# Keeping 1+elu in six of eight hidden pairs and subtracting the weights' sum per output tile

## The chip, the core and the metric

The kernel runs on one core of a Trainium2 chip. The metric is the device time of one execution in microseconds. The engines are called by the profile's names: PE (matrix multiply), PEld (its weight loads), DVE (VectorE), ACT (ScalarE), POOL (GpSimd), SP (the queue that issues the DMAs).

## The reference, cut to what matters

Two small attention steps between 32 inducing points and 4 batches of 12480 tokens of width 128 give a new token array. A feed-forward layer of hidden width 2048 follows, with ELU between its two products:

```python
h = x @ w_in                                              # 49920 x 128 by 128 x 2048
g = np.where(h > 0.0, h, alpha * (np.exp(np.minimum(h, 0.0)) - 1.0))   # elu, alpha = 1
return (g @ w_out).astype(np.float32)                     # 2048 x 128
```

Everything is float32. The feed-forward layer is nearly all of the kernel's time.

## The kernel before

Tokens are cut into blocks: 25 per batch, 15 of 512 tokens and 10 of 480 (`GROUPING`), 100 in all. The hidden width is 16 chunks of 128; two chunks are a pair, and a unit is one pair of one block, so a block is 8 units, cp 0 to cp 7. All 800 units run through one software pipeline, in which each engine's order for PE, DVE and ACT is the order of the code (`tc.manual_schedule`); POOL's and SP's instructions are placed by a scheduler. In loop step n:

- `ffn_in(n)` (L612): two PE matmuls of the unit into a two-bank PSUM tile `ph` (three such tiles rotate). A row of ones in the operand makes this h+1. ACT then writes e = exp(ph-1).
- `ffn_mid(n-1)` (L629): DVE writes g = min(max(ph, 1), e), which is 1+elu(h). For letter D it goes back into `ph`, otherwise into `e`.
- `ffn_split(n-1)` (L636): for P and D, ACT writes `gh`, the reduced-precision (fp32r) copy of g-1.
- `ffn_low(n-2)` (L643): the rest gl = (g-1) - gh. For D one DVE instruction does both; for P, POOL first takes 1 from e (L653) and then takes gh away (L658). For N there is no split, and POOL only takes 1 from e (L653).
- `ffn_out(n-5)` (L660): the second product into the PSUM tile `po` of the block. A split pair takes six fp32r matmuls (gh by `wo_h`, gh by `wo_l`, gl by `wo_h`, for each of two chunks), an N pair two matmuls of full float32 (e by `wo_n`), which the profile records as four. After a block's last unit DVE transposes `po` into `o` (L688), and SP sends it out in four DMAs.

The letters are in `PLAN`, one for each cp: "PDNPDPND". So unit cp 2's second product stands in loop step cp 7 of the same block, and cp 6's in step cp 3 of the next. `gh` and `gl` have four buffers each, `e` five. The steps of the attention for the next blocks and for the next batch (the side work: `scores`, `weights_of`, `gather`, `attend_*`) are put between units at places that fixed numbers give. Before unit 0, and interleaved with units 0 to 12, the weights are taken apart and split into `wo_h`, `wo_l` and `wo_n`.

Of the kernel before, what the change touches and what calls it, by code (L numbers as in the profile page):

```python
# [9 lines left out]
F32 = mybir.dt.float32  # L10
F32R = mybir.dt.float32r
I32 = mybir.dt.int32
U32 = mybir.dt.uint32
AF = mybir.ActivationFunctionType
ALU = mybir.AluOpType
AX = mybir.AxisListType

P = 128
Q = 32
TM = 512  # L20
# [4 lines left out]

PLAN = "PDNPDPND"

# [13 lines left out]
def kernel(  # L45
# [8 lines left out]
    nc = tc.nc  # L54
    B, N, C = x.shape
# [18 lines left out]
    NFC = F // P  # L74
    NCP = NFC // 2
    assert len(PLAN) == NCP
    CHUNKS_S = [f for f in range(NFC) if PLAN[f // 2] != "N"]
    CHUNKS_N = [f for f in range(NFC) if PLAN[f // 2] == "N"]
    WHERE_S = {f: i for i, f in enumerate(CHUNKS_S)}
    WHERE_N = {f: i for i, f in enumerate(CHUNKS_N)}  # L80
    NSPLIT = len(CHUNKS_S)
    SCALE = 1.0 / math.sqrt(C)
# [10 lines left out]
    const = ctx.enter_context(tc.tile_pool(name="const", bufs=1))  # L93
# [4 lines left out]
    ep = ctx.enter_context(tc.tile_pool(name="ep", bufs=2))  # L98
# [7 lines left out]
    op = ctx.enter_context(tc.tile_pool(name="op", bufs=2))  # L106
# [8 lines left out]
    def bank(name, take=False):  # L115
        if not steady and not take:
            return ps_h.tile([P, 2, 512], F32, tag="ph", name=name)[:, 0]
        t = ps_o.tile([P, 512], F32, tag=f"po{turn[0] % 2}", name=name)
        if take:
            turn[0] += 1  # L120
        return t
# [6 lines left out]
        out=fold, in_=ident.rearrange("p (c m) -> p m c", m=Q), axis=AX.X, op=ALU.add  # L128
    )
    sel4 = const.tile([P, 4, Q], F32, name="sel4")  # L130
    for c in range(4):
# [6 lines left out]
        out=mine, in_=ident.rearrange("p (c m) -> p c m", m=Q), axis=AX.X, op=ALU.add  # L138
# [5 lines left out]
    ps = bank("ps_ind")  # L144
# [6 lines left out]
    wo_n = const.tile([P, len(CHUNKS_N), C], F32, name="wo_n")  # L151
    wo_h = const.tile([P, NSPLIT, C], F32R, name="wo_h")
    wo_l = const.tile([P, NSPLIT, C], F32R, name="wo_l")
    WS = 512
    rebias = const.tile([P, 1], F32, name="rebias")
    nc.gpsimd.memset(rebias, -896.0)
# [5 lines left out]
    class Weight:  # L162
# [8 lines left out]
        def take_apart(self):  # L171
            self.part = op.tile([P, WS], U32, tag="o", name="w_part")
            self.scale = self.part.bitcast(F32)
            nc.vector.tensor_scalar(
                out=self.part, in0=self.hi, scalar1=20, scalar2=0x7FF,
                op0=ALU.logical_shift_right, op1=ALU.bitwise_and,
            )
            nc.scalar.activation(self.low, self.lo, AF.Copy, scale=2.0**-52)
# [37 lines left out]
    def load_w_in(half):  # L216
        n = F // 2
        raw = hwp.tile([P, 2 * n], U32, tag="hw", name="w_raw")
        nc.sync.dma_start(raw, w_in[:, 2 * half * n : 2 * (half + 1) * n])
        return [Weight(raw[:, i : i + 2 * WS]) for i in range(0, 2 * n, 2 * WS)]  # L220

    WC = WS // C

    def load_w_out(part, pool, tag):
        raw = pool.tile([P, WC, 2 * C], U32, tag=tag, name="w_raw")
        rows = w_out[part * WS : (part + 1) * WS, :]
        dma = nc.sync.dma_start(raw, rows.rearrange("(c p) d -> p c d", p=P))
        return Weight(raw.rearrange("p c d -> p (c d)")), dma
# [379 lines left out]
    def plan(n):  # L608
        b, k, cp = units[n]
        return PLAN[cp]  # L610

# [24 lines left out]
    def ffn_split(n):  # L636
        v, how = live[n], plan(n)
        shape = list(v["e"].shape)
        if how != "N":
            v["gh"] = ghp.tile(shape, F32R, tag="gh", name=f"gh_{n}")  # L640
            nc.scalar.activation(v["gh"], v["g"], AF.Copy, bias=-1.0)  # L641

    def ffn_low(n):  # L643
        v, how = live[n], plan(n)
        shape = list(v["e"].shape)
        if how == "D":
            v["gl"] = glp.tile(shape, F32R, tag="gl", name=f"gl_{n}")
            nc.vector.scalar_tensor_tensor(  # L648
                out=v["gl"], in0=v["g"], scalar=-1.0, in1=v["gh"].bitcast(F32),
                op0=ALU.add, op1=ALU.subtract,  # L650
            )
        else:
            nc.gpsimd.tensor_scalar(  # L653
                out=v["e"], in0=v["e"], scalar1=-1.0, scalar2=1.0, op0=ALU.add, op1=ALU.mult
            )
        if how == "P":
            v["gl"] = glp.tile(shape, F32R, tag="gl", name=f"gl_{n}")
            nc.gpsimd.tensor_sub(v["gl"], v["e"], v["gh"].bitcast(F32))  # L658

    def ffn_out(n):  # L660
        b, k, cp = units[n]
        v, how = live.pop(n), plan(n)
        T = BLOCKS[k][1]
        U = T // Q
        if cp == 0:
            outs[b, k] = bank(f"po_{b}_{k}", take=True)
        po = outs[b, k]
        parts = []
        for i in range(2):
            f = 2 * cp + i  # L670
            if how == "N":
                parts.append((0, wo_n[:, WHERE_N[f], :], v["e"][:, i]))
            else:
                w = WHERE_S[f]
                parts.append((1, wo_h[:, w, :], v["gh"][:, i]))
                parts.append((1, wo_l[:, w, :], v["gh"][:, i]))
                parts.append((2, wo_h[:, w, :], v["gl"][:, i]))
        parts.sort(key=lambda v: v[0])
        for i, (_, w, g) in enumerate(parts):
            nc.tensor.matmul(  # L680
                po[:, :T], w, g,
                start=(cp == 0 and i == 0),
                stop=(cp == NCP - 1 and i == len(parts) - 1),
            )
        if cp == NCP - 1:
            yield 1
            o = op.tile([P, U, Q], F32, tag="o", name=f"o_{b}_{k}")
            nc.vector.transpose(o.rearrange("p u d -> p (u d)"), po[:, :T])  # L688
            at = b * N + BLOCKS[k][0]
            dst = out[at : at + T, :]  # L690
            for dq in range(4):
                nc.sync.dma_start(
                    dst[:, dq * Q : (dq + 1) * Q].rearrange("(u t) d -> t u d", t=Q),
                    o[dq * Q : (dq + 1) * Q, :, :],
                )
# [45 lines left out]
    def first_batch(b):  # L741
# [8 lines left out]
        win += load_w_in(1)  # L750
        wout = [load_w_out(i, *[(xqp, "xq"), (xmp, "xm")][i // 2]) for i in range(F // WS)]
        steps = {}
# [21 lines left out]
        for s, w in enumerate(win + [w for w, _ in wout]):  # L774
            steps[f"A{s}"], steps[f"C{s}"] = w.take_apart, w.put_together
            steps[f"B{s}"] = lambda w=w, s=s: w.scale_of(s >= 6)
            if s < len(win):
                steps[f"D{s}"] = lambda w=w, s=s: w.finish(win_sb[:, s * WS : (s + 1) * WS])
            else:
# [69 lines left out]
    last = len(units)  # L849
    ffn_mid(last - 1)  # L850
    ffn_split(last - 1)
    ffn_low(last - 2)
    ffn_low(last - 1)
    for n in range(done, last):
        begin(last + n, lambda: ffn_out(n))
        for r in list(running):
            go_on(r, last + n + 1)
# [32 lines left out]
```

## Time and profile before

| | |
|---|---|
| runs, us | 1713.06, 1710.11, 1712.89 (median 1712.89) |
| profiled execution, its own time from first to last instruction | 1710.8 us |
| PE / PEld / DVE / ACT / POOL busy | 97 / 69 / 89 / 81 / 78 % |
| granted PE clock, mean | 0.986 |

The profile gives no other time for the profiled execution than its span; it lies inside the range of the runs. Busy shares are means over a start of about 140 us, in which weights are prepared, and a long even stretch after it, so the prediction reads the even stretch by itself. A row of the timeline has start, duration, engine, line and tiles; PE's matmuls overlap each other, so what one costs is read from start to start and not from its duration.

### The profile page before, as it was taken

The page shows a single profiled execution, that of the slowest core. Times are in us where ns is not written, and L with a number is a line of the kernel's source. Part 1 is how long each engine was busy: PE and PEld are TensorE (multiplying, and loading weights), DVE is VectorE, ACT ScalarE, POOL GpSimd, SP SyncE. Part 2 cuts the span into 40 slices and gives each one's busy share as a digit, 9 for nine tenths or more (in the row PEclk, how much of TensorE's full clock was granted, in tenths as well). Part 3 has the DMA queues.
Part 4 walks back from the last instruction along what each step waited for, and adds up shares of the span by engine and source line. Part 5 has one row for each costly group of instructions (what it writes and reads, how often), then busy time and mean ns, then how long its engine had stood idle before and what let it go on. Part 6 is the DMA issues. An engine that isn't in the chain of part 4 may idle for free.

```text
span 1710.8 us, 22335 instructions
## 1 busy us (share of the span) xinstructions
PE 1656.3 (97%) x7448; PEld 1176.5 (69%) x7448; DVE 1522.5 (89%) x1575; ACT 1390.6 (81%) x1620; POOL 1342.3 (78%) x948
## 2 busy tenths in 40 slices
PE   6589999999999999999999999999999999999998
PEld 4356776677776776767776676677777677777776
DVE  5799899898899998988989999889888989998996
ACT  4378888888787888888888888888878888888886
POOL 4488787787797877877888787787778888888886
PEclk9699999999999999999999999999999999999999
DMA  7144223322324233232223332321222111111111
GB/s 249 35 91 80 56 43 78 63 48 70 70 46 83 37 75 70 45 62 58 71 64 54 65 62 53 75 55 21 74 49 40 35 20 36 28 37 19 36 25 19
DMA packets 384754, 98.10 MB, mean 57 GB/s; under 512 B 364864, under 2 KB 370784, under 8 KB 384384
## 3 DMA queue, kind: packets, MB, share of 16 engines
q1 hardware_dynamic: 384640, 96.68, 27.9%
q8 instruction: 59, 0.97, 0.2%
q14 instruction: 55, 0.45, 0.1%
HBM read 48.94 MB, written 25.56 MB: 44 GB/s over the span
## 4 chain that ended last, share of the span: by engine, by line
PE 87%; DVE 7%; ACT 3%; issue 2%; DMA 1%; POOL 0%; SPq 0%; DVEq 0%; ACTq 0%
PE po L680 62%; PE ph L618 20%; ACT e L626 2%; DVE e L632 1%; PE ps_s L312 1%; PE ps_t L531 1%; PE ps_hh L403 1%; DVE ph L632 1%; ACT gh L641 1%; DMA xm<-in_x_dram 1%; DVE o L688 1%; DVE w_part L198 1%; DVE gl L648 0%; DMA w_raw<-in_moe_w_in_dram 0%; PE ps_hw L467 0%
## 5 line engine op out<-in xcount | busy, mean ns | idle before, releaser
L626 ACT ACTIVATE e<-ph 128x1024 f32<-128x1024 f32 (+1 forms) x800 | 803.4, 1005 | 228.8 <-PE ph L618 223.7
L653 POOL TENSOR_SCALAR e<-e 128x1024 f32<-128x1024 f32 (+1 forms) x500 | 510.8, 1029 | 280.6 <-ACT gh L641 270.4
L658 POOL TENSOR_TENSOR gl<-e,gh 128x1024 fp32r<-128x1024 f32 (+1 forms) x300 | 703.8, 2346 | 16.8
L632 DVE SCALAR_TENSOR_TENSOR e<-ph,e 128x1024 f32<-128x1024 f32 (+1 forms) x500 | 594.5, 1189 | 88.0 <-ACT e L626 84.9
L618 PE MATMUL ph<-stk,hw 128*128 128x512 f32 (+1 forms) x1600 | 566.8, 436 | 15.8 <-DVE e L632 9.6
L680 PE MATMUL po<-gh,wo_h 128*128 128x512 f32 (+1 forms) x1200 | 469.2, 391 | 7.5 <-ACT wo_h L238 3.5
L680 PE MATMUL po<-gh,wo_l 128*128 128x512 f32 (+1 forms) x1200 | 469.3, 391 | 6.6 <-POOL wo_l L239 6.6
L618 PEld LDWEIGHTS ph<-stk,hw 128*128 128x128 f32 x1600 | 295.4, 189 | 188.9 <-issue 84.9
L632 DVE SCALAR_TENSOR_TENSOR ph<-ph,e 128x1024 f32<-128x1024 f32 (+1 forms) x300 | 359.3, 1198 | 63.1 <-ACT e L626 62.3
L680 PE MATMUL po<-gl,wo_h 128*128 128x512 f32 (+1 forms) x1200 | 371.1, 390 | 0.7 <-POOL gl L658 0.7
L680 PE MATMUL po<-e,wo_n 128*128 128x512 f32 (+1 forms) x800 | 367.8, 582 | 0.1
L648 DVE SCALAR_TENSOR_TENSOR gl<-ph,gh 128x1024 fp32r<-128x1024 f32 (+1 forms) x300 | 356.3, 1188 | 1.0 <-ACT gh L641 1.0
L641 ACT ACTIVATE gh<-e 128x1024 fp32r<-128x1024 f32 (+1 forms) x300 | 311.3, 1038 | 13.9 <-DVE e L632 13.5
L641 ACT ACTIVATE gh<-ph 128x1024 fp32r<-128x1024 f32 (+1 forms) x300 | 300.6, 1002 | 19.1 <-DVE ph L632 18.2
L680 PEld LDWEIGHTS po<-gh,wo_h 128*128 128x128 f32 x1200 | 225.9, 188 | 56.6 <-issue 7.4
L680 PEld LDWEIGHTS po<-gh,wo_l 128*128 128x128 f32 x1200 | 225.9, 188 | 56.5 <-POOL wo_l L239 8.2
L680 PEld LDWEIGHTS po<-gl,wo_h 128*128 128x128 f32 x1200 | 225.6, 188 | 49.1 <-POOL gl L658 1.7
L680 PEld LDWEIGHTS po<-e,wo_n 128*128 128x128 f32 x800 | 150.6, 189 | 106.3 <-issue 91.3
L688 DVE STREAM_TRANSPOSE o<-po 128x512 f32<-128x512 f32 (+1 forms) x100 | 69.1, 691 | 4.0 <-PE po L680 4.0
L259 DVE STREAM_TRANSPOSE xT<-xq 128x1024 f32<-128x1024 f32 (+2 forms) x39 | 45.5, 1166 | 0.0
L570 POOL TENSOR_TENSOR s<-s,sm 128x512 f32<-128x512 f32 (+3 forms) x27 | 27.7, 1027 | 19.3 <-DVE sm L569 19.3
L403 PEld LDWEIGHTS ps_hh<-xm,e 128*32 128x32 f32 (+2 forms) x872 | 24.6, 115 | 16.9 <-issue 12.3
(99 smaller groups left out, 557.5 us busy)
## 6 DMA issues: line engine op xcount, KB each, us to landing
xm<-in_x_dram SPq DMA_DIRECT2D x32, 512.0 KB, 4.8
out_dram<-o SPq DMA_DIRECT2D x240, 64.0 KB, 2.0
xq<-in_x_dram SPq DMA_DIRECT2D x84, 128.0 KB, 2.9
out_dram<-o SPq DMA_DIRECT2D x160, 60.0 KB, 2.0
stk<-ahi SPq DMA_DIRECT2D x118, 64.0 KB, 2.0
xq<-in_x_dram SPq DMA_DIRECT2D x60, 120.0 KB, 2.8
stk<-ahi SPq DMA_DIRECT2D x80, 60.0 KB, 2.0
stk<-alo SPq DMA_DIRECT2D x59, 64.0 KB, 2.0
```

The lines of the kernel that those rows point to most:

```text
L259: nc.vector.transpose(t, xq.rearrange("p u d -> p (u d)"))
L403: nc.tensor.matmul(ps[c * Q : (c + 1) * Q, :C], st["e", g][:np_, u * Q : (u + 1) * Q], st["xm", g, u - u % UP][:np_, u % UP, :], start=(u ...
L570: eng.tensor_tensor(out=s, in0=s, in1=sm.unsqueeze(2).broadcast_to([np_, U, Q]), op=ALU.mult)
L618: nc.tensor.matmul(ph[:, i], state[b]["hw"][:, f * P : (f + 1) * P], stacks[b, k], start=True, stop=True,)
L626: nc.scalar.activation(e, ph, AF.Exp, bias=-1.0)
L632: nc.vector.scalar_tensor_tensor(out=v["g"], in0=v["ph"], scalar=1.0, in1=v["e"], op0=ALU.max, op1=ALU.min)
L641: nc.scalar.activation(v["gh"], v["g"], AF.Copy, bias=-1.0)
L648: nc.vector.scalar_tensor_tensor(out=v["gl"], in0=v["g"], scalar=-1.0, in1=v["gh"].bitcast(F32), op0=ALU.add, op1=ALU.subtract,)
L653: nc.gpsimd.tensor_scalar(out=v["e"], in0=v["e"], scalar1=-1.0, scalar2=1.0, op0=ALU.add, op1=ALU.mult)
L658: nc.gpsimd.tensor_sub(v["gl"], v["e"], v["gh"].bitcast(F32))
L680: nc.tensor.matmul(po[:, :T], w, g, start=(cp == 0 and i == 0), stop=(cp == NCP - 1 and i == len(parts) - 1),)
L688: nc.vector.transpose(o.rearrange("p u d -> p (u d)"), po[:, :T])
```

## The change

The letters become "PPNPDPDP": five P, two D and one N, where it was three P, three D and two N. cp 1 and cp 7 go from D to P, cp 6 from N to D. P and N units no longer take 1 from g: gh is the fp32r copy of 1+elu itself, gl = e - gh, and N multiplies 1+elu. What this adds to each output is, per column of the output, the sum of the weights of those twelve chunks. `sum_excess`, called once with block 0's last unit, makes that sum with a matmul of ones by `wo_h`, `wo_l` and `wo_n` and four small DVE reductions. After every DVE transpose POOL subtracts it from `o`, and the DMAs follow that. The chunks of `wo_h` and `wo_l` are sorted P first, so that one slice holds those to be summed.

```diff
-PLAN = "PDNPDPND"
+PLAN = "PPNPDPDP"
...
-    CHUNKS_S = [f for f in range(NFC) if PLAN[f // 2] != "N"]
+    CHUNKS_S = [f for how in "PD" for f in range(NFC) if PLAN[f // 2] == how]
...
+    excess = const.tile([P, Q], F32, name="excess")
...
-            nc.scalar.activation(v["gh"], v["g"], AF.Copy, bias=-1.0)
+            nc.scalar.activation(v["gh"], v["g"], AF.Copy, bias=0.0 if how == "P" else -1.0)
...
-        else:
-            nc.gpsimd.tensor_scalar(
-                out=v["e"], in0=v["e"], scalar1=-1.0, scalar2=1.0, op0=ALU.add, op1=ALU.mult
-            )
         if how == "P":
             v["gl"] = glp.tile(shape, F32R, tag="gl", name=f"gl_{n}")
             nc.gpsimd.tensor_sub(v["gl"], v["e"], v["gh"].bitcast(F32))
+
+    def sum_excess():
+        ones = ep.tile([P, TM], F32, tag="e", name="ones")[:, :P]
+        ones_r = ones.bitcast(F32R)
+        nc.gpsimd.memset(ones, 1.0)
+        n_p = sum(PLAN[f // 2] == "P" for f in CHUNKS_S)
+        n_n = len(CHUNKS_N)
+        parts = [
+            (ones_r, w[:, i : min(i + 4, n_p), :]) for w in (wo_h, wo_l) for i in range(0, n_p, 4)
+        ]
+        parts += [(ones, wo_n[:, i : min(i + 4, n_n), :]) for i in range(0, n_n, 4)]
+        ps = bank("ps_excess")
+        for i, (one, w) in enumerate(parts):
+            m = w.shape[1] * C
+            nc.tensor.matmul(
+                ps[:, :m], one, w.rearrange("p c d -> p (c d)"),
+                start=i == 0, stop=i == len(parts) - 1,
+            )
+        for dq in range(4):
+            rows = slice(dq * Q, (dq + 1) * Q)
+            nc.vector.tensor_reduce(
+                out=excess[rows],
+                in_=ps.rearrange("p (c d) -> p d c", d=C)[rows, rows, :],
+                axis=AX.X, op=ALU.add,
+            )
...
+        if n == NCP - 1:
+            sum_excess()
...
             nc.vector.transpose(o.rearrange("p u d -> p (u d)"), po[:, :T])
+            nc.gpsimd.tensor_tensor(
+                out=o, in0=o, in1=excess.unsqueeze(1).broadcast_to([P, U, Q]), op=ALU.subtract
+            )
```

POOL's order in the last batch, before the change, over eight units from cp 6 on (tile numbers count up with the program):

```order
L653 TENSOR_SCALAR e_13675<-e_13675 128x1024
L658 TENSOR_TENSOR gl_13695<-e_13651,gh_13678 128x1024
L653 TENSOR_SCALAR e_13702<-e_13702 128x1024
L658 TENSOR_TENSOR gl_13739<-e_13702,gh_13720 128x1024
L653 TENSOR_SCALAR e_13733<-e_13733 128x1024
L653 TENSOR_SCALAR e_13750<-e_13750 128x1024
L658 TENSOR_TENSOR gl_13788<-e_13750,gh_13768 128x1024
L653 TENSOR_SCALAR e_13782<-e_13782 128x1024
```

POOL's order after, over one block of the same batch, from the subtraction for block 13 to that for block 14 (`o_14`); `s_3_5` is a tile of the attention:

```order
L713 TENSOR_TENSOR o_13_14159<-o_13_14159,excess 128x512
L655 TENSOR_TENSOR gl_14197<-e_14152,gh_14179 128x1024
L655 TENSOR_TENSOR gl_14225<-e_14192,gh_14207 128x1024
L655 TENSOR_TENSOR gl_14241<-e_14204,gh_14223 128x960
L551 TENSOR_TENSOR s_3_5_14141<-s_3_5_14141,mx_3_5_14249 128x480
L655 TENSOR_TENSOR gl_14258<-e_14220,gh_14239 128x960
L655 TENSOR_TENSOR gl_14288<-e_14255,gh_14272 128x960
L713 TENSOR_TENSOR o_14_14291<-o_14_14291,excess 128x512
```

The five TENSOR_SCALARs of a block are gone, five subtractions for gl stand in place of three (cp 5, 7, 0, 1, 3 in this order), and the subtraction on `o` stands behind that of cp 3.

ACT's order before, around an N pair, with what each instruction waits for (`e` are the exponentials, `gh` the copies):

```order
L626 ACTIVATE e_13533<-ph_13530 128x1024 [waits PE_49,Pool_49]
L641 ACTIVATE gh_13536<-e_13509 128x1024 [waits DVE_49]
L626 ACTIVATE e_13549<-ph_13546 128x1024 [waits PE_49,Activation_49]
L626 ACTIVATE e_13560<-ph_13557 128x1024 [waits PE_49,Pool_49]
L641 ACTIVATE gh_13563<-ph_13546 128x1024 [waits DVE_49]
```

ACT's order after, from the copy of cp 6 to the exponential of the next block's cp 4; the one N pair is `e_14101`:

```order
L642 ACTIVATE gh_14060<-ph_14038 128x1024 [waits DVE_49]
L627 ACTIVATE e_14069<-ph_14066 128x1024 [waits PE_49,Pool_49]
L642 ACTIVATE gh_14072<-e_14057 128x1024 [waits DVE_49,PE_49]
L627 ACTIVATE e_14085<-ph_14082 128x1024 [waits PE_49,Activation_49]
L642 ACTIVATE gh_14088<-e_14069 128x1024 [waits DVE_49,PE_49]
L627 ACTIVATE e_14101<-ph_14098 128x1024 [waits PE_49]
L642 ACTIVATE gh_14104<-e_14085 128x1024 [waits DVE_49,PE_49,Pool_49]
L627 ACTIVATE e_14117<-ph_14114 128x1024 [waits PE_49]
L627 ACTIVATE e_14136<-ph_14133 128x1024 [waits PE_49,Pool_49]
```

Two exponentials in a row, where an N pair has no copy, come once per block instead of twice, so seven units with a copy follow each other; and the copies of cp 7, 0 and 1 now wait for PE as well, because with four buffers for `gh` theirs was last read by the second product of the unit four before.

PE's second product of cp 6, before and then after:

```order
L680 MATMUL po_13_13665<-e_13675,wo_n 128x512 x2
```

```order
L704 MATMUL po_13_14031<-gh_14060,wo_h 128x512
L704 MATMUL po_13_14031<-gh_14060,wo_l 128x512
L704 MATMUL po_13_14031<-gh_14060,wo_h 128x512
L704 MATMUL po_13_14031<-gh_14060,wo_l 128x512
L704 MATMUL po_13_14031<-gl_14074,wo_h 128x512 x2
```

Two float32 matmuls give way to six fp32r ones. The rows of order tell only what stands where, not how long it takes.

## Prediction

> **What bounds the kernel now.** I read the page's busy shares, then the same by stretch, then the waits, then PE's timeline in the last batch, where little side work disturbs it.
>
> ```profile
> span 1710.8 us, 22335 instructions
> PE 1656.3 (97%) x7448; PEld 1176.5 (69%) x7448; DVE 1522.5 (89%) x1575; ACT 1390.6 (81%) x1620; POOL 1342.3 (78%) x948
> ...
> 60.00:120.00 60.00, 37.07 (x115) 22.40 (x113) 54.20 (x61) 38.13 (x57) 42.57 (x39) 0.80 0.43 84
> ...
> 200.00:1600.00 1400.00, 1392.82 (x6182) 993.47 (x6182) 1265.58 (x1277) 1177.29 (x1346) 1124.97 (x773) 1.00 0.27 54
> ...
> ACT e L626 <- PE ph L618: 223.7, 235, 2.6
> PE ph L618 <- DVE e L632: 9.6, 12, 2.7
> ```
>
> The stretch rows give length, then busy time of PE, PEld, DVE, ACT, POOL. From 200 to 1600 us PE is busy 99.5%, at full clock; from 60 to 120 us, where the weights are prepared, it is DVE (54.2 of 60) and not PE. In the waits ACT stands idle 223.7 us for PE's `ph`, and PE only 9.6 us for DVE. So after the start PE sets the pace. Busy time flatters PE, whose matmuls overlap, so I check by start times (start, duration):
>
> ```profile
> 1501.38 0.62 PE L618 MATMUL ph<-stk,hw 128*128 128x512 f32 x2
> 1501.84 1.88 PE L680 MATMUL po<-e,wo_n 128*128 128x512 f32 x4
> 1503.16 1.03 PE L618 MATMUL ph<-stk,hw 128*128 128x512 f32 x2
> 1504.03 0.39 PE L680 MATMUL po<-gh,wo_h 128*128 128x512 f32 x1
> ...
> 1505.42 0.62 PE L618 MATMUL ph<-stk,hw 128*128 128x512 f32 x2
> ...
> 1506.58 0.40 PE L680 MATMUL po<-gh,wo_l 128*128 128x512 f32 x1
> ...
> 1507.29 0.62 PE L618 MATMUL ph<-stk,hw 128*128 128x512 f32 x2
> ...
> 1509.14 0.62 PE L618 MATMUL ph<-stk,hw 128*128 128x512 f32 x2
> ...
> 1699.83 0.38 PE L680 MATMUL po<-gh,wo_h 128*128 128x480 f32 x1
> ...
> 1701.15 0.38 PE L680 MATMUL po<-gh,wo_h 128*128 128x480 f32 x1
> ...
> 1702.46 1.77 PE L680 MATMUL po<-e,wo_n 128*128 128x480 f32 x4
> ...
> 1704.29 0.38 PE L680 MATMUL po<-gh,wo_l 128*128 128x480 f32 x1
> ```
>
> A step with a split pair's second product takes 1.86 us ((1509.14 - 1505.42) / 2): 8 matmuls at 0.233, no gap. A step with an N pair and one with a split pair take 1505.42 - 1501.38 = 4.04, so the N step takes 2.18, **0.32 more**. At 480 tokens the last steps, which have no `ph`, show it bare: a split product 1701.15 - 1699.83 = 1.32; the N product from 1702.46 to the next one's start, which is a matmul (0.22) before 1704.29, so 1.61, **0.29 more**. An N product's four records thus take 1.72 us for 512 tokens, and six fp32r matmuls 1.40.
>
> The Trainium skill (Perfetto Trace Analysis, Identifying the Most-Contended Engine) says that PE's headroom is to be judged by the busy share of weight loads, not of matmuls. By that PE, at 69%, would have room and its time would not count; the trace disagrees, since the starts above leave no gap and ACT's waits end on PE.
>
> **The change, part by part.** Means from the groups between 200 and 1600 us (busy, mean ns of one), in which 692 exponentials are 86.5 blocks of 16.18 us:
>
> ```profile
> L641 ACT ACTIVATE gh<-e 128x1024 fp32r<-128x1024 f32 (+1 forms) x259 | 269.0, 1039 | 9.1 <-DVE e L632 8.6
> L554 ACT ACTIVATE s<-s 128x512 f32<-128x512 f32 (+3 forms) x24 | 14.8, 615 | 0.0
> L589 ACT CAST ahi<-aT 128x512 fp32r<-128x512 f32 (+3 forms) x24 | 14.4, 601 | 0.0
> L381 ACT ACTIVATE s<-s,bias 128x512 f32<-128x512 f32 (+3 forms) x20 | 14.2, 708 | 0.0
> L322 ACT COPY s<-ps_s 128x480 f32<-128x480 f32 (+3 forms) x18 | 10.2, 568 | 0.0
> L565 ACT ACTIVATE sm<-sm,eps 128x16 f32<-128x16 f32 (+3 forms) x24 | 7.2, 301 | 0.0
> ...
> L658 POOL TENSOR_TENSOR gl<-e,gh 128x1024 fp32r<-128x1024 f32 (+1 forms) x259 | 607.9, 2347 | 14.5
> L653 POOL TENSOR_SCALAR e<-e 128x1024 f32<-128x1024 f32 (+1 forms) x433 | 442.3, 1029 | 243.9 <-ACT gh L641 236.2 <-PE po L680 2.7
> L591 POOL TENSOR_TENSOR alo<-aT,ahi 128x512 fp32r<-128x512 f32 (+3 forms) x24 | 30.4, 1266 | 0.0
> L550 POOL TENSOR_TENSOR s<-s,mx 128x512 f32<-128x512 f32 (+3 forms) x24 | 24.6, 1026 | 1.1 <-DVE mx L549 1.1
> ...
> L648 DVE SCALAR_TENSOR_TENSOR gl<-ph,gh 128x1024 fp32r<-128x1024 f32 (+1 forms) x259 | 307.9, 1189 | 0.0
> ...
> 1505.22 1.01 ACT L641 ACTIVATE gh<-ph 128x1024 fp32r<-128x1024 f32 x1
> 1506.12 1.03 ACT L626 ACTIVATE e<-ph 128x1024 f32<-128x1024 f32 x1
> 1507.02 1.06 ACT L641 ACTIVATE gh<-e 128x1024 fp32r<-128x1024 f32 x1
> ...
> 1513.18 0.62 PE L618 MATMUL ph<-stk,hw 128*128 128x512 f32 x2
> 1513.91 1.03 ACT L626 ACTIVATE e<-ph 128x1024 f32<-128x1024 f32 x1
> 1514.96 1.23 DVE L632 SCALAR_TENSOR_TENSOR e<-ph,e 128x1024 f32<-128x1024 f32 x1
> ...
> 1516.89 0.62 PE L618 MATMUL ph<-stk,hw 128*128 128x512 f32 x2
> ...
> 1705.59 0.68 DVE L688 STREAM_TRANSPOSE o<-po 128x480 f32<-128x480 f32 x1 [4.05 <-PE po L680]
> ```
>
> - PE, cp 6 split: 60 blocks x 0.32 + 40 x 0.29 = 30.8 off, on the path. Block 0's falls in the start, where PE is not the bound, so 30.5.
> - ACT, one copy more per block: 0.90 by start to start (1506.12 - 1505.22; the 1.04 of the row overlaps its neighbour). Over the stretch 1177.3 + 78 of 1373 us, 91%. Nothing on the path while PE covers it: exponential and copy take 1.80, PE's step 1.86.
> - DVE, one gl less per block (D three to two): -1.19, 1265.6 - 103 = 1163, 85%. Off the path.
> - POOL, five TENSOR_SCALARs off (-5.15 per block), two gl more (+4.69), the subtraction on `o` more. The last is not in the trace; the nearest are the broadcast subtraction L550 (1.03) and the plain one L591 (1.27), both of half a gl's size. I take 1.03, since its operands are as L550's. Per block 5 x 2.35 + 1.03 = 12.8, with the attention's 0.95 (L591, L550 and as much again for its product) 13.7 of 15.9, 86%. Off the path, except once:
> - The end: after the last transpose (1705.59, 0.68) the subtraction stands ahead of the last four DMAs: 1.0 at 480 tokens and a handoff of about 0.1, so +1.1 (bounds 1.0 to 1.4). Elsewhere the DMAs only leave later, and the two `o` tiles are used again two blocks on.
> - `sum_excess`: on PE 4 x 0.233 + 2 x 0.12 and 256 columns of float32, half of an N matmul's 0.86, so 1.6; the four small reductions on DVE run beside the next product. It stands where block 0 ends, when PE has just become the bound: +1.6 (0 to 3).
> - The start itself: POOL loses 1.03 for each P or N unit and gains two gl of 2.35 ahead of the last split of `w_out`; DVE, the busy one there, loses two gl. One wait that PE has there shows the size (start, duration, idle before):
>
> ```profile
> 99.87 0.50 PE L680 MATMUL po<-gh,wo_l 128*128 128x512 f32 x1 [4.12 <-POOL wo_l L239]
> ```
>
>   It may vanish (-4.1), or a like one of two gl may come (+4.7). I take 0.
> - Waits of PE: a `ph` tile that D holds comes free late, and the unit two after the one behind D takes that one's tile. The rows show it: `ph` at 1513.18 is cp 5, behind D; DVE frees it at 1516.19; PE takes it again at 1516.89, 0.70 later. ACT may thus be 0.70 behind there without PE noticing. After the change D stands at cp 4 and 6 instead of 1, 4 and 7, so there are two such places, not three, and the second has the N product's 0.32 more. The new wait of the copies of cp 7, 0 and 1 for PE falls where it costs nothing: the fourth gh matmul ends at 1506.98 (1506.58 + 0.40) and the copy begins by its own pace at 1507.02. I take 0; the bounds are -9.6, all of PE's present waits for DVE, and the first rival.
>
> Sum: -30.5 + 1.6 + 1.1 = **-27.8**, so a span of 1683.0. The profiled 1710.8 lies 2.1 below the median of 1712.89, and I carry the difference over: **1685**.
>
> **Rivals.** (1) ACT takes the pace. It now gets back only 0.90 (no copy at cp 2) and 0.32 per block, half of before, and its side work (the five other ACT rows, 60.8 us) falls between seven units that leave 0.06 each. One such operation of 0.5 to 0.6 fits into the 0.70; two in one run do not. If a fifth came through, 12 us: 1697. If all came through, 61: 1746, **slower than before**; it turns slower once more than 28 of the 61 do. Against it: between 200 and 1600 us PE also has side work, in which ACT catches up, and D's tight places are fewer. (2) POOL is late. cp 7, 0 and 1 are three gl in a row at 2.35 against PE's 1.86, 1.0 behind at the end; the exponential of the unit five later needs that `e` tile. From a `ph` start the copy ends at 1.86 + 0.73 + 0.90 + 1.06 = 4.55, gl at 4.55 + 1.0 + 2.35 = 7.9, the need at 5 x 1.86 + 0.7 = 10.0, so 2.1 remain, and one attention step of 1.0 to 1.3 fits. If each of some 25 blocks lost 1 us: 1710. The bound as a whole would go to POOL only with a gl above 2.77, at 15.9 per block. The Trainium skill (GPSIMD Reference, Engine selection) advises VectorE for two-input elementwise work, GpSimd being about 2x slower; the rows agree (2347 against 1189), and it matters only if this rival holds. (3) PE's matmul time is not the pace and something else that the change leaves alone is: then the 30.5 do not come, only +2.7 remains, and 1715.6 cannot be told from no change; the starts without gaps speak against it. This is what the Trainium skill's rule on weight loads (Perfetto Trace Analysis, Identifying the Most-Contended Engine) would make of PE's 69%. (4) The start loses over 10 us.
>
> **Chances.** Mine 0.80, with its own range 1678 to 1692 (start -4 to +5, waits -3 to +3). Rival 1 in part (1690 to 1709) 0.08, in full and slower 0.04; rival 2 0.04, most of it faster than before; rival 3 0.02; rival 4 or another loss 0.02. A measurement of this kernel can tell about 0.2% (3.4 us). Faster 0.92, same 0.03, slower 0.05. The range 1677 to 1697 holds the first and part of the second.
>
> **What would show it.** The steady stretch should have every step at 1.86 but one of 2.18 per block, ACT about 91%, POOL 86%, DVE 85% busy, and ACT's waits for `ph` cut from 224 to some 130 us. I am wrong if PE's waits for DVE at `ph` grow past 20 us (rival 1), if exponentials wait for POOL (rival 2), or if the steps are as short as said and the time is not.

## The result, and the profile after

The changed kernel takes **1693.37 us** (median of 4 runs, 1692.92 to 1693.46) against 1711.50 of the kernel before (1710.05 to 1713.06, 4 runs with those shown above): 18.1 us faster, ratio 0.9894, 95% interval 0.9879 to 0.9908. Forecast were 1685 and a gain of 27.8. So the sign and the mechanism came, and a third of the size did not. The profiled execution has a span of 1691.5, 19.2 below that of before (from the unrounded spans).

The page of after, its span and its busy shares:

```profile
span 1691.5 us, 23388 instructions
PE 1627.5 (96%) x7656; PEld 1216.0 (72%) x7656; DVE 1428.5 (84%) x1479; ACT 1478.7 (87%) x1720; POOL 1421.0 (84%) x751
```

The same by stretch (length, then busy time of PE, PEld, DVE, ACT, POOL; granted clock, DMA share, GB/s):

```profile
60.00:120.00 60.00, 34.88 (x99) 22.69 (x100) 47.86 (x53) 32.81 (x50) 36.00 (x31) 0.73 0.37 73
...
200.00:1600.00 1400.00, 1390.44 (x6451) 1041.88 (x6450) 1200.95 (x1209) 1274.81 (x1455) 1213.62 (x610) 1.00 0.28 54
```

From 200 to 1600 us ACT is busy 1274.8 / 1400 = 91.1%, POOL 86.7%, DVE 85.8%; forecast were 91, 86 and 85. PE has no room there (99.3%, and 99.5% before). From 60 to 120 us PE, DVE, ACT and POOL all do *less* than before (PE 34.9 against 37.1, DVE 47.9 against 54.2, POOL 36.0 against 42.6): that stretch waits for something. The waits (us in total, times, longest):

```profile
ACT e L627 <- PE ph L619: 121.4, 159, 5.1
...
PE ph L619 <- DVE e L633: 15.9, 16, 5.0
```

ACT's waits for `ph` fell from 223.7 to 121.4 (forecast: some 130), and PE's waits for DVE stay under the 20 us at which the prediction would have been wrong. PE's timeline in the last batch shows the steps:

```profile
1481.85 0.63 PE L619 MATMUL ph<-stk,hw 128*128 128x512 f32 x2
1483.71 0.63 PE L619 MATMUL ph<-stk,hw 128*128 128x512 f32 x2
1485.57 0.63 PE L619 MATMUL ph<-stk,hw 128*128 128x512 f32 x2
1486.04 1.88 PE L704 MATMUL po<-e,wo_n 128*128 128x512 f32 x4
...
1489.61 0.62 PE L619 MATMUL ph<-stk,hw 128*128 128x512 f32 x2
```

A step with a split pair is 1.86 (1485.57 - 1483.71), and an N step and a split one together are 4.04 (1489.61 - 1485.57), to the hundredth what they were; there is now one N step per block. The end is as forecast too: the subtraction stands between the last transpose and the last DMAs.

```profile
1685.10 0.68 DVE L712 STREAM_TRANSPOSE o<-po 128x480 f32<-128x480 f32 x1 [4.88 <-PE po L704]
1685.86 1.20 POOL L713 TENSOR_TENSOR o<-o,excess 128x480 f32<-128x480 f32 x1 [3.06 <-DVE o L712]
1687.09 1.93 SPq L719 DMA_DIRECT2D out_dram<-o  x4
```

**Where the time went.** I take the start of each block's first `ph` matmul from the timelines of both kernels and subtract. The difference to before grows by these amounts (us; minus is faster):

| | up to block 0 | block 0 to 2 | block 2 to 99 | block 99 to the end | sum |
|---|---|---|---|---|---|
| forecast | 0 | +1.6 | -29.9 | +0.5 | -27.8 |
| after | -3.0 | **+9.1** | **-26.0** | +0.6 | -19.2 |

The forecast's columns are its own terms put at their places. The second product of a block's cp 6 stands in the next block. So before block 2 there is only block 0's, which the forecast left out, and `sum_excess` (+1.6); blocks 1 to 97 come between 2 and 99, 59 of 512 tokens at 0.32 and 38 of 480 at 0.29; the last two blocks (-0.58) and the subtraction (+1.1) come behind. The -3.0 is not the change's: block 0 begins at 66.3 us in the profiled execution of before and at 62.9 to 64.0 in all others but e6's, among them the one of e4 below, which differs from before in one letter of the plan. The runs of before lie at 1710.1 and at 1712.9 to 1713.1, and the profiled one belongs by its span to the longer ones. So two places remain. The start lost 7.5 more than I said, and the long stretch gained 3.9 less.

The start's loss can be read step by step, from one unit's first `ph` matmul to the next. At unit 11, cp 3 of block 1, after stands as far ahead of before as at block 0 (3.1 against 3.0). The step from there takes 8.61 instead of 2.11, before first:

```profile
105.00 0.62 PE L618 MATMUL ph<-stk,hw 128*128 128x512 f32 x2
...
107.11 1.03 PE L618 MATMUL ph<-stk,hw 128*128 128x512 f32 x2
```

```profile
101.86 0.73 PE L619 MATMUL ph<-stk,hw 128*128 128x512 f32 x2 [0.56 <-DVE e L633]
...
110.47 1.05 PE L619 MATMUL ph<-stk,hw 128*128 128x512 f32 x2
```

The step behind it, in which the sum stands, takes 5.96 instead of 3.56. That is 6.5 and 2.4; all the rest up to block 2 comes to 0.2.

The experiments go by these columns. Between kernels whose edits do not touch it, the long stretch repeats within 0.4 and the end within 0.1; the first two columns vary by about 1, and e6's first by 3; the medians vary by 1 to 2 us.

### The profile page after: what moved, and what is told of

Same layout as the page of the kernel before. It is cut to its first block, busy times and chain, and to the rows that moved or that the text cites. A ratio compares the mean times of both kernels' runs of the same rounds, so it can differ in the third digit from the quotient of the medians.

```text
span 1691.5 us, 23388 instructions
## 1 busy us (share of the span) xinstructions
PE 1627.5 (96%) x7656; PEld 1216.0 (72%) x7656; DVE 1428.5 (84%) x1479; ACT 1478.7 (87%) x1720; POOL 1421.0 (84%) x751
## 4 chain that ended last, share of the span: by engine, by line
PE 72%; DVE 9%; ACT 7%; issue 6%; POOL 2%; DMA 2%; SPq 0%; POOLq 0%; DVEq 0%; ACTq 0%
PE po L704 51%; PE ph L619 17%; ACT e L627 4%; DVE e L633 3%; ACT gh L642 3%; POOL gl L655 1%; PE ps_t L532 1%; DVE xT L260 1%; DVE gl L649 1%; PE ps_s L313 1%; DVE ph L633 1%; PE ps_hh L404 1%; DMA xm<-in_x_dram 1%; DMA out_dram<-o 1%; DVE o L712 1%
## 5 line engine op out<-in xcount | busy, mean ns | idle before, releaser
L655 POOL TENSOR_TENSOR gl<-e,gh 128x1024 fp32r<-128x1024 f32 (+1 forms) x500 | 1169.5, 2355 | 213.2 <-ACT gh L642 201.6
L627 ACT ACTIVATE e<-ph 128x1024 f32<-128x1024 f32 (+1 forms) x800 | 800.8, 1002 | 122.8 <-PE ph L619 121.4
L633 DVE SCALAR_TENSOR_TENSOR e<-ph,e 128x1024 f32<-128x1024 f32 (+1 forms) x600 | 714.6, 1193 | 184.5 <-ACT e L627 178.6
L704 PE MATMUL po<-gh,wo_h 128*128 128x512 f32 (+1 forms) x1400 | 547.6, 391 | 11.1 <-ACT wo_h L239 6.8
L704 PE MATMUL po<-gh,wo_l 128*128 128x512 f32 (+1 forms) x1400 | 547.8, 391 | 2.6 <-POOL wo_l L240 2.6
L642 ACT ACTIVATE gh<-e 128x1024 fp32r<-128x1024 f32 (+1 forms) x500 | 518.6, 1037 | 27.5 <-DVE e L633 25.5
L633 DVE SCALAR_TENSOR_TENSOR ph<-ph,e 128x1024 f32<-128x1024 f32 (+1 forms) x200 | 239.5, 1198 | 30.2 <-ACT e L627 28.4
L649 DVE SCALAR_TENSOR_TENSOR gl<-ph,gh 128x1024 fp32r<-128x1024 f32 (+1 forms) x200 | 237.4, 1187 | 0.1
L642 ACT ACTIVATE gh<-ph 128x1024 fp32r<-128x1024 f32 (+1 forms) x200 | 201.1, 1005 | 4.3 <-DVE ph L633 3.9
L704 PE MATMUL po<-e,wo_n 128*128 128x512 f32 (+1 forms) x400 | 184.0, 582 | 0.0
L713 POOL TENSOR_TENSOR o<-o,excess 128x512 f32<-128x512 f32 (+1 forms) x100 | 126.6, 1266 | 4.4 <-DVE o L712 4.4
```

Source lines behind the costliest of these rows:

```text
L627: nc.scalar.activation(e, ph, AF.Exp, bias=-1.0)
L633: nc.vector.scalar_tensor_tensor(out=v["g"], in0=v["ph"], scalar=1.0, in1=v["e"], op0=ALU.max, op1=ALU.min)
L642: nc.scalar.activation(v["gh"], v["g"], AF.Copy, bias=0.0 if how == "P" else -1.0)
L649: nc.vector.scalar_tensor_tensor(out=v["gl"], in0=v["g"], scalar=-1.0, in1=v["gh"].bitcast(F32), op0=ALU.add, op1=ALU.subtract,)
L704: nc.tensor.matmul(po[:, :T], w, g, start=(cp == 0 and i == 0), stop=(cp == NCP - 1 and i == len(parts) - 1),)
L713: nc.gpsimd.tensor_tensor(out=o, in0=o, in1=excess.unsqueeze(1).broadcast_to([P, U, Q]), op=ALU.subtract)
```

## The experiments

The same table for all of them, with the median of each; before has 1710.3 to 1710.8 in these comparisons. Ratios and intervals stand with each experiment.

| | median | up to block 0 | 0 to 2 | 2 to 99 | 99 to end |
|---|---|---|---|---|---|
| after | 1693.37 | -3.0 | +9.1 | -26.0 | +0.6 |
| e1 no sum | 1690.99 | -2.9 | +7.2 | -26.3 | +0.6 |
| e2 N at cp 6, D at cp 2 | 1698.68 | -2.4 | +7.7 | -18.8 | +0.6 |
| e3 two N | 1715.05 | -2.5 | +6.2 | -2.5 | +1.3 |
| e4 before, cp 6 split | 1750.02 | -2.3 | +2.6 | +38.5 | -0.2 |
| e6 sum by quarter | 1694.26 | +0.1 | +8.2 | -26.1 | +0.6 |
| e9 three gl on DVE | 1688.57 | -2.4 | +2.5 | -26.0 | +0.6 |
| e10 last quarter early | 1688.38 | -2.6 | +3.7 | -26.0 | +0.6 |
| e11 = e6 + e10 | 1688.78 | -2.8 | +3.4 | -25.9 | +0.6 |
| e12 hn on ACT | 1692.86 | -2.3 | +8.5 | -26.5 | +0.6 |
| e13 = e9 + e10 + e12 | 1687.97 | -2.4 | +2.4 | -26.3 | +0.6 |
| e14 = e10 + e12 | 1686.81 | -3.4 | +2.4 | -26.5 | +0.7 |
| e15 = e10, product of hn later | 1685.33 | -2.7 | +3.6 | -28.5 | +0.6 |

### The two halves of the change: e3 and e4

e3 keeps everything of the change except the split of cp 6; e4 takes the split of cp 6 alone, on the kernel before.

```diff
 e3, from the changed kernel             e4, from the kernel before
-PLAN = "PPNPDPDP"                      -PLAN = "PDNPDPND"
+PLAN = "PPNPDPNP"                      +PLAN = "PDNPDPDD"
```

> The changed kernel with letters PPNPDPNP: cp 6 is left unsplit as before, while 1+elu, the sum, the subtraction from the output and the move of cp 1 and 7 from VectorE to GpSimd stay. Theory A: PE's steps are those of before, the relief of DVE and POOL is worth nothing, the sum costs some 2.4 us and the subtraction at the end 1.2: 1713 to 1716 against 1711.5 before. Rival D (the relief of DVE and POOL, not PE's shorter product, brought the gain): 1700 or less.

e3: 1715.05 (1714.74 to 1716.16), ratio 1.0027 [1.0017, 1.0038]. Per block POOL has five tensor_scalars less and two gl more, and DVE two gl less. This gains 2.5 us in the long stretch, of the 26.0 that the whole change gains there, and the start and the end take more than that back: the relief by itself is worth nothing.

> The kernel before with one edit, letters PDNPDPDD: cp 6 split on VectorE, nothing of 1+elu. PE's step at cp 6 is 0.32 us shorter, but DVE gets 1.14 us more per block: 14.6 + 1.1 = 15.8 of the 15.9 that PE then needs. Theory A (PE alone counts as long as the others keep up): DVE just does not keep up, some 1705, between 1690 and 1715. If only PE counted: 1686. If DVE is fully the bound: above 1711.

e4: 1750.02 (1748.99 to 1751.18), ratio 1.0232 [1.0217, 1.0248]. The split alone makes the kernel slower by 2.3%, worse than I expected. Its windows and waits say why:

```profile
200.00:1600.00 1400.00, 1359.73 (x6221) 992.05 (x6220) 1322.51 (x1334) 1231.56 (x1397) 1019.92 (x670) 1.00 0.27 53
```

```profile
PE ph L618 <- DVE gl L648: 37.3, 49, 3.1
```

DVE is busy 94.5% there and PE only 97.1%: four D pairs per block are more than DVE can do beside its side work, and PE now waits for gl. The two halves do not add (+4.8 and +39.8 by the medians, about -18 together); each needs the other.

### Where the one N stands: e2

```diff
-PLAN = "PPNPDPDP"
+PLAN = "PPDPDPNP"
```

> The changed kernel with letters PPDPDPNP: the one unsplit pair stands at cp 6 and not at cp 2, with D at cp 2 and 4; same counts of everything. Theory A: block 0's cp 6 no longer needs the split of the last quarter, so 3 to 5 us of the start come back and the even stretch stays at 0.3 us per block below before: 1688 to 1690. Rival B (the sum is the whole loss): 1693. Rival C (ACT's side work is tuned to the place of the unsplit pair, so that moving it costs in the even stretch): 1696 or more.

e2: 1698.68 (1698.35 to 1699.62), ratio 0.9933 [0.9918, 0.9948]: 5.3 slower than the changed kernel, where theory A had 1688 to 1690. The same letters in another order make the same matmuls, and in blocks without side work (78 to 98, for example) the block times of the two agree within 0.05. Between blocks 2 and 99 e2 loses 10.1 us in 30 blocks with side work, 0.15 to 1.06 in each, and gets 3 back in others: 7.2. So the time of rival C came: there is little room for side work, and which unit the N step stands at decides whether it hides. In the changed kernel it did hide, nearly. The three largest losses, 1.05 each in blocks 22, 47 and 72, come with the wait of rival 2 of the prediction and not of rival 1: an exponential on ACT waits for POOL's gl, which none does in the trace of the changed kernel. Four us later PE waits for the product `hw_l`, which DVE makes from a copy that ACT makes. In block 22:

```profile
455.81 0.97 ACT L627 ACTIVATE e<-ph 128x960 f32<-128x960 f32 x1 [1.06 <-POOL gl L655]
...
459.78 1.06 PE L532 MATMUL ps_t<-xT,hT 128*32 128x512 f32 x8 [0.71 <-DVE hw_l L480]
```

That the one wait leads to the other is likely by the order of ACT's work, but no run shows it, and the other 27 blocks were not taken apart. The start went against theory A as well: with cp 6 unsplit it lost 7.7 in place of 9.1, so 1.4 came back and not 3 to 5.

### The sum: e1 and e6

e1 puts a constant in place of the sum (its outputs keep the share of the weights' sum); e6 makes it in four parts of 256 columns, one behind each second unit of block 0.

```diff
-        ones = ep.tile([P, TM], F32, tag="e", name="ones")[:, :P]
...
+        nc.gpsimd.memset(excess, 0.0)                 # e1
```

```diff
-        if n == NCP - 1:
-            sum_excess()
...
+        if n < NCP and n % 2:                         # e6, after ffn_out
+            sum_excess(n // 2)
```

> The changed kernel without the matmuls and reductions that sum the weights: excess is set to zero by one memset, so every output keeps a constant too much. Theory A (the even stretch gains its 0.3 us per block as forecast; the start loses about 8 us, of which some 5 are block 0's cp 6, now split, waiting for the last quarter of w_out, and about 2.4 the sum on PE): 1690 to 1691 against 1693.4, and the wait for wo_h and wo_l at cp 6 stays. Rival B (the sum is the whole loss of the start): 1685. Rival C (the loss lies in the even stretch, in ACT or POOL): 1693.

e1: 1690.99 (1690.77 to 1691.24), ratio 0.9887 [0.987, 0.9903]. The sum costs 2.4 by the medians and 1.9 by the column, where I had 1.6. The timeline and the granted clock of that place show the rest, after first and then e9:

```profile
111.33 1.27 PE L670 MATMUL ps_excess<-wo_h,ones 128*128 128x512 f32 x3
112.39 1.24 PE L670 MATMUL ps_excess<-wo_l,ones 128*128 128x512 f32 x3
```

```profile
111.30:114.10 2.80, 2.80 (x10) 2.32 (x9) 0.00 (x1) 1.97 (x2) 0.43 (x1) 0.61 0.45 133
```

```profile
106.19 0.74 PE L671 MATMUL ps_excess<-wo_h,ones 128*128 128x512 f32 x3
106.77 0.74 PE L671 MATMUL ps_excess<-wo_l,ones 128*128 128x512 f32 x3
```

```profile
106.15:107.95 1.80, 1.80 (x10) 1.53 (x9) 0.21 (x1) 1.50 (x2) 0.00 (x0) 1.00 0.50 152
```

Three of these matmuls have 1280 columns. In after they take 1.06 from start to start, at a granted clock of 0.61; in e9, where PE had waited less just before, 0.58 at 1.00, which is the 0.233 per 512 columns I had reckoned with. So PE's clock was lower behind the longer waits, and the sum paid for that. e2 shows the same one unit earlier, where PE had waited 2.40 for `wo_n`: the N product takes 3.78, where it takes 1.88 at full clock.

```profile
106.22 3.78 PE L704 MATMUL po<-e,wo_n 128*128 128x512 f32 x4 [2.40 <-ACT wo_n L236]
```

```profile
106.20:110.00 3.80, 3.79 (x5) 1.73 (x6) 3.42 (x4) 2.42 (x5) 3.50 (x4) 0.50 0.42 67
```

The Trainium skill (TensorE: Matmul & The Clock Gate, Terms) describes a monitor that gates PE's clock by how busy PE is; these rows agree.

> The sum is made in four parts, each behind a product of block 0 (cp 1, 3, 5, 7), so that only the last quarter and the four reductions stand where block 0 ends. Taking the sum away altogether gave 1691.0 against 1693.4. Theory A: those 2.4 us are PE's time for the seven matmuls at a place where PE has become the bound, and three quarters of them hide in PE's waits for the weights: 1691 to 1692. Rival B: the loss is the handing over (ones, the reductions, excess before the first subtraction) or PE is the bound all through block 0: 1693 to 1694, no different from the changed kernel.

e6: 1694.26 (1691.46 to 1695.34), ratio 0.99 [0.9885, 0.9914]: not told apart from the changed kernel by time. Between block 0 and 2 it saves 1.0, but its profiled execution reached block 0 3.1 us later than after's. That is a spread of the start and not the edit: e11, which has the same edit, reaches it at 63.5. One us is the most I can claim for it.

### The last quarter of `w_out`: e9, e10, e11

Here the timeline of after has the loss in the open. PE's two rows come first, then POOL's (the bracket is the idle time before, and what ended it):

```profile
105.06 0.50 PE L704 MATMUL po<-gh,wo_h 128*128 128x512 f32 x1 [2.47 <-ACT wo_h L239]
108.17 0.79 PE L704 MATMUL po<-gh,wo_l 128*128 128x512 f32 x1 [2.62 <-POOL wo_l L240]
```

```profile
103.03 4.67 POOL L655 TENSOR_TENSOR gl<-e,gh 128x1024 fp32r<-128x1024 f32 x2 [0.98 <-ACT gh L642]
107.66 1.73 POOL L240 TENSOR_TENSOR wo_l<-w_raw,wo_h 128x128 fp32r<-128x128 f32 x4
```

Two gl in a row, those of units 8 and 9, stand ahead of the last `wo_l`, and PE waits for it. Before the change unit 9 was a D pair, whose gl DVE made, and the last quarter had two chunks to split instead of four, for which PE did not wait:

```profile
107.79 0.89 POOL L239 TENSOR_TENSOR wo_l<-w_raw,wo_h 128x128 fp32r<-128x128 f32 x2
```

A second thing delays the same quarter after the change. A step of its preparation on DVE starts 0.18 after another gl on POOL, takes 2.48 and ends 0.28 after that gl; in e10 it takes 0.57, and in before 0.57 too. `wo_h` and `wo_l` are made from its result, so both of PE's waits come behind it. After first, then e10:

```profile
97.28 2.38 POOL L655 TENSOR_TENSOR gl<-e,gh 128x1024 fp32r<-128x1024 f32 x1 [0.96 <-DMA xq<-in_x_dram]
```

```profile
97.46 2.48 DVE L203 TENSOR_SCALAR w_raw<-w_raw 128x512 uint32<-128x512 uint32 x1
```

```profile
95.61 0.57 DVE L203 TENSOR_SCALAR w_raw<-w_raw 128x512 uint32<-128x512 uint32 x1
```

It looks like the delay that hn meets further below. e9 gives three gl of the start back to DVE; e10 leaves them on POOL and prepares the last quarter one and two units earlier (u7 is unit 7; C7, D7 and E7 are its steps).

```diff
+            eng = nc.vector if n in (1, 7, 9) else nc.gpsimd          # e9
-            nc.gpsimd.tensor_sub(v["gl"], v["e"], v["gh"].bitcast(F32))
+            eng.tensor_sub(v["gl"], v["e"], v["gh"].bitcast(F32))
```

```diff
-    D6 A7 u6 B7 E6 u7 u8 C7 D7 u9 u10 E7 u11 u12
+    D6 A7 u6 B7 E6 u7 C7 D7 u8 E7 u9 u10 u11 u12                      # e10
```

> gl of units 1, 7 and 9 alone (cp 1 and 7 of block 0, cp 1 of block 1) is made by VectorE as before the change; all later units are left as they are. Theory A: about 4 us of the loss in the start come from GpSimd, which got two more gl of 2.35 us ahead of the last split of w_out, so that PE waits for wo_h and wo_l (2.5 and 2.6 us): 1689 to 1690. Rival B: VectorE is the engine that sets the pace of the start (54 of 60 us busy before), so that three gl more on it cost what GpSimd gains: 1693 to 1696.

e9: 1688.57 (1687.28 to 1688.92), ratio 0.9867 [0.9853, 0.9882].

> Only the order of the start is changed: the third and fourth quarter's steps C7 D7 and E7 of the preparation come one unit and two units earlier (E6 u7 C7 D7 u8 E7 u9 in place of E6 u7 u8 C7 D7 u9 u10 E7). Theory A: PE's waits for wo_h and wo_l of the last quarter (2.47 + 2.62 us) are a true loss that the earlier preparation removes in part: 1689 to 1691. Rival B: DVE, ACT and POOL are full there, and what comes earlier pushes the units back by as much: 1693 to 1695.

e10: 1688.38 (1687.71 to 1689.87), ratio 0.9869 [0.9854, 0.9884].

Each takes 5 us off, at the place named: the loss between block 0 and 2 falls from 9.1 to 2.5 and to 3.7, and no other column moves by more than 0.6. In e10 both waits are gone, and POOL's rows, the first block below, show the splits ahead of the two gl. In e9 the waits shrink to 1.65 and 0.89, the second block:

```profile
101.69 1.72 POOL L240 TENSOR_TENSOR wo_l<-w_raw,wo_h 128x128 fp32r<-128x128 f32 x4
103.38 4.79 POOL L655 TENSOR_TENSOR gl<-e,gh 128x1024 fp32r<-128x1024 f32 x2
```

```profile
103.09 0.49 PE L705 MATMUL po<-gh,wo_h 128*128 128x512 f32 x1 [1.65 <-ACT wo_h L239]
104.47 0.50 PE L705 MATMUL po<-gh,wo_l 128*128 128x512 f32 x1 [0.89 <-POOL wo_l L240]
```

The long step of 8.61 is 1.87 in e10 and 4.90 in e9, and the one behind it, with the sum, 4.6 in both instead of 5.96: part of the 5 us is the sum at full clock. Both edits also free DVE's step of the last quarter (0.57 in e10, 0.43 in e9), so they do not tell the two gl ahead of `wo_l` from the gl that held DVE up. That cp 6 is now split is the smaller part: it is worth 2.9 in this column between e3 and the changed kernel, and 2.6 in e4. e3, with the gl on POOL and cp 6 unsplit, loses 6.2, of which the sum is some 2.

> Both edits: the sum by quarters and the last quarter of w_out prepared earlier. If each removes its own loss the gains add up: 1687 to 1689. If both only move the same wait, no better than the better one of them: 1690 to 1692. If neither helps, 1693 to 1695.

e11: 1688.78 (1687.59 to 1689.97), ratio 0.9872 [0.9855, 0.9888]: no better than e10. That the quartered sum has nothing left to hide in once the wait is gone is my reading; no run shows it apart.

### The rest of the long stretch: e12 to e15

Block by block from 2 to 99, after gains 0.25 to 0.35 in nearly all, and the shortfall lies at few places. The largest comes three times, in the step after cp 7 of blocks 21, 46 and 71, which is 1.09 *longer* than before. There DVE makes hn, a 128x128 product of the attention, and PE needs it next. The groups of DVE between 200 and 1600 us (busy, mean ns of one, idle before) and the timeline at block 21, before:

```profile
L450 DVE TENSOR_SCALAR hn<-h,r 128x128 f32<-128x128 f32 x3 | 0.9, 287 | 0.1
```

```profile
445.36 2.03 POOL L653 TENSOR_SCALAR e<-e 128x960 f32<-128x960 f32 x2
...
446.25 0.29 DVE L450 TENSOR_SCALAR hn<-h,r 128x128 f32<-128x128 f32 x1
```

and after (the last row is PE's):

```profile
L451 DVE TENSOR_SCALAR hn<-h,r 128x128 f32<-128x128 f32 x3 | 4.1, 1375 | 0.1
```

```profile
445.05 0.68 PE L619 MATMUL ph<-stk,hw 128*128 128x480 f32 x2
...
445.81 2.21 POOL L655 TENSOR_TENSOR gl<-e,gh 128x960 fp32r<-128x960 f32 x1
446.73 1.38 DVE L451 TENSOR_SCALAR hn<-h,r 128x128 f32<-128x128 f32 x1
448.16 0.30 PEld L457 LDWEIGHTS ps_ht<-sel,hn 128*128 128x128 f32 x2 [1.59 <-DVE hn L451]
```

The same instruction takes 0.287 before and 1.375 after, and the 1.09 between them is what the step got longer. It starts in the middle of a gl on POOL and ends at 448.11, 0.09 after that gl (448.02). The Trainium skill (SBUF — State Buffer, Who interferes with whom) says that DVE and GpSimd share one pair of ports under an exclusive lock, taken for a whole instruction by whichever starts first, and that a tensor_scalar on DVE can need it; the rows agree. Before the change POOL ran two tensor_scalar passes there instead, of 1.0 each, and the first of them ended 0.10 after hn began. In these rows hn's time goes by how long POOL's instruction still has to run. The first batch's hn shows it beside one and the same instruction, a product of two full tiles. In before (first block) that runs another 0.89, and hn takes 0.97 and ends 0.08 after it; in e3 it runs another 0.09, and hn takes 0.29. No hn starts early in a tensor_scalar pass, so whether one would hold it up is not shown.

```profile
52.15 1.29 POOL L212 TENSOR_TENSOR win_sb<-w_raw,w_part 128x512 f32<-128x512 f32 x1 [2.84 <-DVE r L443]
...
52.55 0.97 DVE L450 TENSOR_SCALAR hn<-h,r 128x128 f32<-128x128 f32 x1
```

```profile
49.57 1.29 POOL L213 TENSOR_TENSOR win_sb<-w_raw,w_part 128x512 f32<-128x512 f32 x1 [2.84 <-DVE w_raw L209]
...
50.77 0.29 DVE L451 TENSOR_SCALAR hn<-h,r 128x128 f32<-128x128 f32 x1
```

e12 lets ACT make hn:

```diff
-        nc.vector.tensor_scalar_mul(hn, st["h"], st["r"])
+        nc.scalar.activation(hn, st["h"], AF.Copy, scale=st["r"])
```

> Only norm_h is changed: the 128x128 product hn = h x r, once per batch, is made by ScalarE instead of VectorE. In the trace of the changed kernel VectorE's instruction for it takes 1.375 us instead of 0.287 before the change, and ends 0.09 us after the end of a gl on GpSimd that runs beside it; PE then waits for hn. Theory A: VectorE is held off while GpSimd's two-input instruction runs, and three times (the blocks 21, 46, 71) PE loses 1.1 us by it: ScalarE takes some 0.3 us for it and the time falls by 3, to 1690 to 1691, with the step after cp 7 of these blocks 1.1 us shorter. Rival B: PE's wait there is the place of the step, whatever engine makes hn (the reciprocal before it comes late behind ph and e): 1693 to 1694.

e12: 1692.86 (1692.66 to 1694.94), ratio 0.9896 [0.9881, 0.9912]. A miss: the step got 0.16 shorter. The timeline shows what took the place of the lock: ACT's order puts a copy of gh ahead of hn.

```profile
444.83 0.68 PE L619 MATMUL ph<-stk,hw 128*128 128x480 f32 x2
...
446.48 0.96 ACT L642 ACTIVATE gh<-ph 128x960 fp32r<-128x960 f32 x1
...
447.33 0.40 ACT L451 ACTIVATE hn<-h,r 128x128 f32<-128x128 f32 x1
...
447.78 0.49 PE L457 MATMUL ps_ht<-sel,hn 128*128 128x128 f32 x2 [0.66 <-DMA out_dram<-o]
```

hn takes 0.40 on ACT but ends 2.90 after the step's `ph` (447.73 - 444.83), against 3.06 on DVE (448.11 - 445.05): the 0.16. (The bracket of PE's row names a DMA, but PE starts 0.05 after hn's end.) Who makes it changes little; when PE asks for it was still open.

> Three edits together: gl of units 1, 7 and 9 by VectorE, the last quarter of w_out prepared earlier, and hn by ScalarE. The first two each gave 5 us at the same wait of PE, so by theory A they do not add (1688), and hn takes 3 more: 1684.5 to 1686. If the start's two edits add in part: 1682 to 1684. Rival B, if VectorE is full in the start and the two get in each other's way and hn gives nothing: 1688 to 1691.

> The last quarter of w_out prepared earlier and hn by ScalarE, gl of all five pairs left to GpSimd. By theory A the two losses are far apart in time and add up: 5.0 + 3, 1685 to 1686. If hn gives nothing: 1688 to 1689.

e13: 1687.97 (1686.47 to 1689.12), ratio 0.9866 [0.9849, 0.9884]; e14: 1686.81 (1685.82 to 1688.31), ratio 0.9859 [0.9843, 0.9875]. In e13 the edits of the start do not add, as expected, since they remove the same wait (+2.4 against +2.5 for e9 alone); the time missed its 1684.5 to 1686 because hn gave nothing. Neither gets the 3 us of hn; e14's lead over e10 is within what the medians of like kernels differ by.

e15 is e10 with PE's product of hn one unit later, and hn left on DVE:

```diff
-        steps.append((end + 0.8, lambda: spread_h(b), f"h{b}"))
+        steps.append((end + 0.925, lambda: spread_h(b), f"h{b}"))
```

> On top of the last quarter prepared earlier (1688.4) one step is moved: PE's product of hn (ps_ht), once per batch, comes one unit later; hn stays on VectorE at its place, where it takes 1.38 us beside GpSimd's gl. ScalarE's hn had taken 0.40 us but started behind a copy of gh, so it came hardly earlier and gave 0.16 us per batch: that left open whether the 1.1 us per batch are PE's wait for hn. Theory A: they are, and a unit later hn is there in time: the step after cp 7 of the blocks 21, 46 and 71 gets 1.0 to 1.1 us shorter and nothing is lost at the next one: 1685 to 1685.5. Rival B: VectorE's loss of 1.1 us itself holds up the units behind it, or the product waits as long one unit later: no change, 1688 to 1689.

e15: **1685.33** (1684.74 to 1687.30), ratio 0.9855 [0.9839, 0.9872]. Its timeline at block 21, hn and PE's product of it:

```profile
441.15 1.41 DVE L451 TENSOR_SCALAR hn<-h,r 128x128 f32<-128x128 f32 x1
...
443.35 0.38 PE L457 MATMUL ps_ht<-sel,hn 128*128 128x128 f32 x2
```

hn is as slow as ever (1.41), and PE no longer waits for it. The three steps get 1.61 shorter each, the two steps behind them 0.73 longer (0.62 + 0.11), so 2.6 of the shortfall of 3.9 come back (2.5 by the column). Most of the loss was PE's wait: with hn as slow as before the edit, 0.88 of the 1.09 of each batch are gone, so the delay on DVE costs at most the other 0.21 when nobody stands behind it. e15 is the fastest version here, 25 us below before and 8 below the changed kernel.

## Why the prediction was right, and where its sum was off

- **PE sets the pace, and an N pair costs 0.32 us more than a split one.** Right: steps of 1.86 and 2.18 on both sides, and PE busy 99.3% of the long stretch. Rival 3 (PE's time is not the pace) is dead; e3, without the split, gains 2.5 of the 26.0 in the long stretch and nothing in all.
- **The copies on ACT, gl on POOL and DVE lie off the path.** Right: 91.1, 86.7 and 85.8% against 91, 86 and 85, ACT's waits 121.4 against 130. The subtraction is 1.29 at 512 tokens, the price of the plain subtraction L591 (1.30) and not, as I took it, of the broadcast one L550 (1.05); it costs only what lies at the end.
- **The end, +1.1**: 1.20 for the subtraction itself; the column has +0.6 where +0.5 was forecast, and e3, whose cp 6 is unsplit, has the end's cost bare, +1.3. Right.
- **`sum_excess`, +1.6**: mis-sized; 1.9 to 2.4, by the clock of 0.61 that I had taken as full.
- **The start, 0 with bounds -4.1 and +4.7**: this is the term that was mis-sized most, and the loss of 7.5 lies beyond its upper bound. The wait of 4.12 that I showed for it was for the third quarter's split, not the last (for the last PE did not wait before the change). It did vanish, but PE waited elsewhere instead, so that at unit 11 nothing was won. I named the other mechanism at its upper bound, "a like one of two gl may come", and took the middle. It did come: PE waited 2.47 + 2.62 for the last quarter, with two gl ahead of its `wo_l` and DVE's step of it held up beside another gl, and moving the gl or the quarter gives 5 back (e9, e10). The middle was not the likeliest value: in POOL's order two gl stand right ahead of the last split. That a gl on POOL can hold DVE up was in no term. With the wait eased (e9) the column is +2.5 against +1.6; the 0.9 between them was not taken apart.
- **Waits of PE, 0 (bounds -9.6 to rival 1)**: too good by 3.9 in the long stretch; 2.6 of it is PE's wait for hn, which was late beside a gl (e15). The remaining 1.3 nets out small gains and losses of up to 1.1 in a few blocks per batch around the side work, which I did not take apart.
- **Rivals 1 and 2**, ACT and the side work, POOL late: not in the long stretch of this kernel, but one place away. e2, with the N at cp 6, loses 7.2 in blocks with side work; 3.1 of it come with an exponential that waits for POOL, and the rest is open between the two.

Put together: -29.9 came as -26.0, the start's +1.6 as +9.1, and before's profiled execution had itself begun block 0 some 2.5 us late. Of the 9.7 us of gain that are missing by the medians, 5 are PE's wait in the start, the clock under the sum included, and 2.6 its wait for hn; 1.4 are the median of before, which came down from 1712.89 to 1711.50 with its fourth run; 0.7 is not assigned. e15, which takes out both waits, lies at 1685.33, where 1685 was forecast; with terms of 1 us still open that closeness is in part luck.

## What to carry to other kernels

A pace set by one engine can be priced from start to start to a few hundredths of a us, and that price held in nearly all of 97 blocks; what went wrong were the seams, where the weights are still being prepared and where one small instruction feeds PE. When work moves to another engine's queue, look at what it now stands ahead of there and what it now runs beside, and take the bound that this gives rather than the middle. Two changes that each lose alone can win together, when one makes the room that the other uses.

## What the runs showed of the hardware that I had not expected

- One DVE instruction took 0.287, 0.97 or 1.375 us by how long the GpSimd instruction beside it still had to run (0.1, 0.89 or 1.29), and the longer ones ended 0.08 to 0.09 after GpSimd's. A larger one took 2.48 instead of 0.43 to 0.57, in the path of the weights' preparation.
- PE's matmuls behind two waits of 2.5 and 2.6 us ran at a granted clock of 0.61, 1.06 us for 1280 columns against 0.58 at 1.00, and behind one of 2.40 in e2 at 0.50, so work put at the end of a stretch of waits costs more than its steady price.
- GpSimd's subtraction of a broadcast tile of 128x512 took 1.05 us in one form (L550, one value for each run of 32 neighbours) and 1.29 in the other (L713, the same 32 values repeated), the same as with two full tiles (1.30).
